# Seven block products in place of eight for the input products of seven expert groups, with weight bounds on ScalarE and the weight clamp on GpSimd

## The chip, the cores and the metric

The kernel runs on one core of a Trainium2 chip. The metric is the device time of one execution, in microseconds. In the profile PE is TensorE's matmul, PEld its weight load, DVE VectorE, ACT ScalarE, POOL GpSimd and SP SyncE.

## What is computed

```python
# 4 x 8 heads, 576 positions, 64 wide; log_f = log(clip(f, 1e-4, 1)), cum = cumsum(log_f)
scores = q @ k.T / 8 + cum[:, None] - cum[None, :]          # causal
x = softmax(scores) @ v                                     # -> 2304 tokens x 512
h = ((x @ w_a) * (x @ w_b)) @ w_out                         # 512 -> 1536 -> 512
u = h @ w_in                                                # 512 -> 2048
g = where(u >= 1, u, where(u <= -1, 0, (u + 1) ** 2 / 4))
out = g @ w_out2                                            # 2048 -> 512
```

All inputs are float32, and the weights come to 68 units of 128 x 512 values, seen by the kernel as pairs of 32-bit words.

## The kernel before, in words

**Precision.** A factor of a matmul in the two expert layers is kept as two float16 parts, high and low. A product is then three matmuls (`mm3`): high x high, high x low and low x high. Tokens are the moving columns, weights the stationary 128 x 128 blocks. The inputs of a layer stand in `xhl` (high `xh`, low `xl`; 4 blocks of 128 rows, 2304 columns), the layer's result is gathered in `y` in float32.

**Groups.** The first layer has six groups of 256 of its 1536 inner columns. A group uses six units of weights: four for the input products (`w_a`, `w_b`), two for the output products. The second layer has four groups of 512 inner columns, with four input and four output units. Group 0 of the first layer is done batch by batch among the attention; its last batch and all other groups make up the late part, which is planned and issued by itself (`late`).

**Items.** In the late part a group goes over the tokens in five spans of 460 or 464 columns (`WSPANS`). An item makes the input products of a span, turns them into activations (for the first layer scale on ScalarE, product on VectorE; for the second clamp on VectorE, square on ScalarE, maximum on VectorE; then on both a float16 copy and its float32 image on ScalarE and the low part by a subtraction on GpSimd, tile `al`), and leaves its output products pending, to be put among the input products of the next item. Output products are added into `y` by VectorE.

**Weights.** `weight_stream` makes float16 parts of the weights two units at a time: a load, magnitude and low word on ScalarE, a clamp, a shift and a combining instruction on VectorE, an addition on GpSimd (`decode`, tile `wm`); then the largest magnitude by VectorE (`wmx`), its square, a matmul with ones and a scale (`norm`); then high part on ScalarE, scaling and low part on GpSimd (`split_unit`), for output units also a scaled-down copy on VectorE. Two `wm` tiles alternate, and finished units lie in rings, input and output ones apart, whose slots come free after a group's last span.

**Order.** The class `Plan` collects all instructions with their dependences (a matrix of PSUM counts as one bank), ranks them by modelled durations, and issues each engine's list in the order that its simulated clock gives; it models that GpSimd and some VectorE instructions exclude each other. Each engine then works through its list in order. All instructions are issued from one line of that class, so every row of the profile names L326 and tiles tell them apart; tiles of the late part have an l in front.

Of the kernel before, what the change touches and what calls it, by code (L numbers as in the profile page):

```python
# [31 lines left out]
WIDE = 464  # L32
# [5 lines left out]
WSPANS = [(460 * i, 460) for i in range(4)] + [(1840, 464)]  # L38
# [5 lines left out]
RI2, RO2 = 4, 4  # L44
LT = 2
# [15 lines left out]
def weight_order():  # L61
    order = []
    for f0, f1 in G1:
        for f in range(f0, f1):
            for n in ("moe_w_a", "moe_w_b"):
                order += [(n, kc, f) for kc in range(KC)]
# [281 lines left out]
def tile_decay_attention__then__moe__then__moe2(  # L348
# [9 lines left out]
    nc.nc_inputs = {qk.tensor.name, v.tensor.name, f.tensor.name, w.tensor.name}  # L358
# [11 lines left out]
    ring_i = Ring(pool("ring_i", 1), RI)  # L370
# [35 lines left out]
    ysc = const.tile([P, len(WSPANS)], F32, name="ysc")  # L406
    yinv = const.tile([P, len(WSPANS)], F32, name="yinv")
# [91 lines left out]
    free = {"in": RI, "out": RO, "next": 0}  # L499
    slots = {"in": [ring_i] * RI, "out": [ring_o] * RO}  # L500
    rings = {"in": slots["in"][:], "out": slots["out"][:]}
    split = {"in": 0, "out": 0}

    def kind(u):
        n = len(G1) * 6
        return "in" if (u % 6 if u < n else (u - n) % 8) < 4 else "out"
# [32 lines left out]
    def norm(sq, inv, sc):  # L539

        bp = psum_t()
        nc.tensor.matmul(bp[:, 0:2], lhsT=unit, rhs=sq, start=True, stop=True)
        nc.vector.tensor_scalar(inv.bitcast(I32), bp[:, 0:2].bitcast(I32), 1, 0x3F800000, ALU.logical_shift_right,
                                ALU.bitwise_and)
        nc.gpsimd.tensor_scalar(inv, inv, 2.0 ** 49, 2.0 ** -76, ALU.mult, ALU.max)
# [9 lines left out]
    def decode(u, m):  # L555
# [10 lines left out]
        nc.vector.tensor_scalar(m, m, F64_MIN, F64_MAX, ALU.max, ALU.min)  # L566
# [9 lines left out]
    def split_unit(u, m):  # L576
# [4 lines left out]
        p = slot(k)  # L581
        hi = p.tile([P, UB, P], F16, name=f"whi_{k}", tag=f"whi_{k}")
        lo = p.tile([P, UB, P], F16, name=f"wlo_{k}", tag=f"wlo_{k}")
# [10 lines left out]
        yield True  # L594

    def weight_stream():
# [5 lines left out]
        for u0 in range(0, NU + 2, 2):  # L602
# [7 lines left out]
            if scaled:  # L610
                norm(sq, winv[:, cols], wsc[:, cols])
                yield True
            if u0 > 0:
                for j in range(2):
                    yield from split_unit(u0 - 2 + j, old[:, j])
            if u0 < NU:
                mx = const2.tile([P, 2], F32, name="wmx", tag="wmx")
                nc.vector.tensor_reduce(mx, new, axis=AX.X, op=ALU.max, apply_absolute_value=True)
                sq = const2.tile([P, 2], BF16, name="wsq", tag="wsq")
                nc.scalar.activation(sq, mx, AF.Square)  # L620
# [13 lines left out]

    def w_free(u):
# [3 lines left out]
        free[kind(u)] += 1  # L639
# [16 lines left out]
    def act_pair(nt):  # L656
        return tuple(env["act"].tile([P, env["width"]], F16, name=n, tag=n)[:, :nt] for n in ("ah", "al"))
# [39 lines left out]
    def group1(g):  # L697

        if ("g", g) not in xw:
# [4 lines left out]
            for i in range(2):  # L704
                nc.gpsimd.tensor_tensor(q[:, 2 * i:2 * i + 2], winv[:, u + 2 * i:u + 2 * i + 2], inv, ALU.mult)
                nc.gpsimd.tensor_scalar(r[:, i:i + 1], q[:, 2 * i:2 * i + 1], q[:, 2 * i + 1:2 * i + 2], 2.0 ** -22,
# [4 lines left out]
    def out_scale1(g, b):  # L711
        if ("o", g, b) not in xw:
            u = base1[g] // UB + 4
            t, o = small("ot", 2), small("os", 2)
            nc.gpsimd.tensor_scalar(t, group1(g)[0], xinv[:, b:b + 1], 2.0 ** 31, ALU.mult, ALU.mult)
            nc.gpsimd.tensor_scalar(t[:, 0:1], t[:, 0:1], t[:, 1:2], 2.0 ** -4, ALU.mult, ALU.mult)
# [4 lines left out]
    def group2(g):  # L721
        if ("k", g) not in xw:
# [3 lines left out]
            nc.vector.tensor_scalar(k, k, 2.0 ** 36, None, ALU.mult)  # L726
# [3 lines left out]
    def moe1_item(g, b, c0, nt, last_use):  # L730
# [5 lines left out]
        def epilogue(oa, ob, r):  # L736
# [3 lines left out]
            nc.scalar.activation(asb, oa, AF.Copy, scale=2.0 ** -26)  # L740
# [34 lines left out]
        def accumulate(c, o, sc):  # L775
            ys = y[:, c, cs]
            if g == 0:
                nc.scalar.activation(ys, o, AF.Copy, scale=sc)
                return
            nc.vector.scalar_tensor_tensor(ys, o, sc, ys, ALU.mult, ALU.add)  # L780
            if g == len(G1) - 1:
                nc.vector.tensor_reduce(ymx[:, c:c + 1], ys, axis=AX.X, op=ALU.max, apply_absolute_value=True)
                if c == KC - 1:
                    finish(ymx)

        def finish(ymx):
            i = WSPANS.index((c0, nt))
            mx = const2.tile([P, 1], F32, name="ymx", tag="ymx")
            box = []
            nc.vector.tensor_reduce(mx, ymx, axis=AX.X, op=ALU.max)  # L790
            after(4, lambda: box.append(top_of(mx, 1)))
            after(9, lambda: spread(box[0], 1, yinv[:, i:i + 1], ysc[:, i:i + 1]))
# [517 lines left out]
```

## Time and profile before

| | |
|---|---|
| median of 3 runs | 1010.12 us (1008.34 to 1010.54) |
| profiled execution | 1009.84 us |
| its span, first to last instruction | 1008.1 us |
| granted TensorE clock, mean over the span | 0.997 |
| TensorE, VectorE, ScalarE, GpSimd busy | 99%, 68%, 59%, 62% |
| late part | 260 to 1004.3 us |

A matmul's record lasts longer than the time until the next one starts, since matmuls overlap; from start to start is what one takes. A duration of VectorE or GpSimd holds the time for which the instruction was held up inside the engine.

### The profile page before, as it was taken

To read this page: it belongs to the slowest core of one execution; us is meant where nothing else is said; L and a number is where in the kernel's file an instruction comes from. 1 tells how busy PE (TensorE), PEld (TensorE's weight loads), DVE (VectorE), ACT (ScalarE), POOL (GpSimd) and SP (SyncE) were. 2 spreads that over 40 slices of the span, in tenths; PEclk is the share of its full clock that TensorE was granted. 3 is DMA by queue.
4 is the path that set the end of the run, shared out by engine and by line. 5 is a ranking of instruction groups with operands and counts; after the bars stand their busy time and mean duration, and the time that the engine had idled before them with its cause. 6 is when DMAs were issued, how large, how long until landed. Compare 5 with 4: busy or idle time off the path is not lost.

```text
span 1008.1 us, 18407 instructions
## 1 busy us (share of the span) xinstructions
PE 993.8 (99%) x6877; PEld 585.7 (58%) x6877; DVE 689.0 (68%) x1570; ACT 594.9 (59%) x1137; POOL 620.8 (62%) x743
## 2 busy tenths in 40 slices
PE   8999999999999999999999999999999999999998
PEld 6888788888754555555555555454555555555554
DVE  7998988778553753755635778987566688487443
ACT  6899989877653442434524445777564556364342
POOL 7689988984672642644624645658574587278321
PEclk8999999999999999999999999999999999999999
DMA  8765555420120210211101121011111112010112
GB/s 230 193 200 157 153 165 160 141 76 10 42 64 21 84 43 1 84 43 42 61 24 42 64 63 43 22 63 38 47 42 42 42 43 63 22 42 11 48 57 76
DMA packets 22114, 72.17 MB, mean 72 GB/s; under 512 B 2772, under 2 KB 5332, under 8 KB 21960
## 3 DMA queue, kind: packets, MB, share of 16 engines
q1 hardware_dynamic: 22024, 70.99, 23.3%
q8 instruction: 54, 0.88, 0.4%
q14 instruction: 36, 0.29, 0.1%
HBM read 60.41 MB, written 5.96 MB: 66 GB/s over the span
## 4 chain that ended last, share of the span: by engine, by line
PE 88%; ACT 4%; DVE 4%; POOL 2%; issue 1%; DMA 0%; ACTq 0%; POOLq 0%; DVEq 0%
PE lmm L326 73%; PE mm L326 4%; PE s L326 4%; PE tp L326 3%; PE o L326 3%; ACT prob L326 1%; ACT th L326 1%; DVE prob L326 1%; DVE tl L326 1%; PE mm L1192 1%; DVE wm L326 1%; POOL qk L326 1%; POOL q L326 0%; DVE xt L326 0%; POOL wm L326 0%
## 5 line engine op out<-in xcount | busy, mean ns | idle before, releaser
L326 POOL TENSOR_TENSOR lal<-ltmp,ltmp 128x460 f16<-128x460 f32 (+2 forms) x134 | 162.1, 1218 | 208.9 <-ACT ltmp L326 192.6
L326 PE MATMUL lmm<-xhl,lwhi_in 128*128 128x460 f16 (+1 forms) x800 | 215.4, 357 | 0.0
L326 PE MATMUL lmm<-xhl,whi_in 128*128 128x460 f16 (+2 forms) x704 | 183.6, 351 | 0.9 <-ACT y L326 0.6
L326 PEld LDWEIGHTS <-whi_in 128*128 128x128 f16 x896 | 86.7, 98 | 70.3 <-issue 2.3
L326 PEld LDWEIGHTS <-lwhi_in 128*128 128x128 f16 x800 | 77.8, 97 | 75.5
L326 DVE TENSOR_SCALAR wm<-wm 128x512 f32<-128x512 f32 (+1 forms) x136 | 93.4, 691 | 33.7 <-ACT wm L326 32.6
L326 PE MATMUL lmm<-lah,lwhi_out 128*128 128x460 f16 (+1 forms) x360 | 115.5, 358 | 0.0
L326 PE MATMUL lmm<-lah,lwlo_out 128*128 128x460 f16 (+1 forms) x360 | 114.8, 358 | 0.0
L326 PE MATMUL lmm<-lal,lwdown 128*128 128x460 f16 (+1 forms) x360 | 114.7, 357 | 0.0
L326 PE MATMUL lmm<-xhl,lwlo_in 128*128 128x460 f16 (+1 forms) x400 | 114.3, 357 | 0.0
L326 POOL TENSOR_TENSOR wm<-wm,wr 128x512 int32<-128x512 int32 x68 | 90.8, 1335 | 36.5 <-DVE wm L326 24.9
L326 ACT ACTIVATE ltmp<-ltmp,lhmid,lihalf 128x460 f32<-128x460 f32 (+1 forms) x80 | 59.9, 766 | 89.8 <-DVE ltmp L326 85.3
L326 ACT ACTIVATE lah<-ltmp 128x460 f16<-128x460 f32 (+2 forms) x134 | 76.6, 578 | 56.1 <-DVE ltmp L326 47.5
L326 DVE SCALAR_TENSOR_TENSOR y<-lmm,los,y 128x460 f32<-128x460 f32 (+1 forms) x100 | 68.2, 692 | 50.3 <-PE lmm L326 50.2
L326 PE MATMUL lmm<-xhl,wlo_in 128*128 128x460 f16 (+2 forms) x352 | 98.5, 351 | 0.0
L326 DVE TENSOR_SCALAR ltmp<-lmm,lhtop,lhlow 128x460 f32<-128x460 f32 (+1 forms) x80 | 58.8, 751 | 52.7 <-PE lmm L326 47.7
L326 ACT ACTIVATE prob<-prob,nm 128x256 f32<-128x256 f32 (+4 forms) x144 | 79.8, 588 | 9.6 <-DVE nm L326 9.4
L326 DVE SCALAR_TENSOR_TENSOR tl<-tp,th 128x384 f16<-128x384 f32 (+2 forms) x128 | 71.4, 567 | 11.0 <-ACT th L326 9.8
L326 ACT ACTIVATE ltmp<-lmm 128x460 f32<-128x460 f32 (+2 forms) x54 | 29.3, 542 | 82.5 <-PE lmm L326 82.3
L326 ACT ACTIVATE ltmp<-lah 128x460 f32<-128x460 f16 (+2 forms) x134 | 75.3, 576 | 2.1
L326 ACT ACTIVATE wr<-wraw 128x512 int32<-128x512 uint32 x68 | 45.8, 673 | 52.1 <-POOL wm L326 51.9
L326 DVE SCALAR_TENSOR_TENSOR ltmp<-lmm,lgr,ltmp 128x460 f32<-128x460 f32 (+2 forms) x54 | 36.2, 680 | 56.5 <-PE lmm L326 52.6
(170 smaller groups left out, 2258.8 us busy)
## 6 DMA issues: line engine op xcount, KB each, us to landing
wraw<-in_w_dram SPq DMA_DIRECT2D x68, 512.0 KB, 3.6
raw<-in_qk_dram SPq DMA_DIRECT2D x26, 608.0 KB, 4.0
vraw<-in_v_dram SPq DMA_DIRECT2D x16, 320.0 KB
qk<-q SPq DMA_DIRECT2D x28, 160.0 KB, 2.4
out_dram<-ltmp SPq DMA_DIRECT2D x16, 230.0 KB, 2.0
y<-in_qk_dram SPq DMA_DIRECT2D x2, 608.0 KB
cum_d<-xhl SPq DMA_DIRECT2D x1, 1216.0 KB
out_dram<-ltmp SPq DMA_DIRECT2D x4, 232.0 KB, 2.0
```

Of the source, the lines that this page charges most:

```text
L326: getattr(getattr(self.nc, engine), method)(*a, **kw)
L1192: nc.heat = lambda: tc.nc.tensor.matmul(heat, lhsT=mask[:, 0:P], rhs=mask[:, 0:512 - HALF], start=False, stop=False, skip_group_check=True)
```

## The change

**Seven products.** The input products of first-layer groups 2 to 5 and second-layer groups 1 to 3 are made by the Strassen-Winograd scheme (`s_set`). A pair of input units is a 2 x 2 arrangement of blocks (two inner blocks by two halves of the 512 rows), and the tokens of an item form the other 2 x 2 arrangement: the same row halves by two column halves, a left one of 384 tokens in the first 1152 and a right one of 384 in the second. Eight block products become seven, of sums of blocks. The sums of weights are made in `split_pair` (four additions on VectorE, more columns of high and low parts), those of the inputs in `x_sums`, once for the first layer during group 1 and once for the second during its group 0; one of them overwrites its place in `xhl`. In a set two partial sums are kept in PSUM: bank X is copied to bank Y by ScalarE while TensorE makes another product in V; V is copied to SBUF by ScalarE; VectorE writes X plus that copy into Z, later into V; TensorE goes on adding into X, Y and Z. The other late groups use `plain_set`, with the same items.

**Items of 768 tokens.** There are three items a group, each two halves of 384 columns, in place of five spans. Seven PSUM banks serve matmuls and one the small transposes and bounds, before six and two. The first layer's two halves of activations share a tile; 18 such tiles and 8 temporaries stand in the late part, before 8 and 8 of single parts and 6.

**Bounds and clamp.** From unit 8 on, a weight's bound is the root of its sum of squares, by ScalarE with an accumulated output, in place of VectorE's maximum, and the clamp of a decoded weight runs on GpSimd. The bound of `y` is likewise from squares. For pairs one bound holds for both units. Scale constants change with that, and one multiplication by 0.25 is added per batch in `xscale`.

**Buffers.** Late input weights lie in four pair tiles (one in place of the early input ring), output units in five slots instead of six.

```diff
-WIDE = 464
+SH = 384
...
-WSPANS = [(460 * i, 460) for i in range(4)] + [(1840, 464)]
+NI = NT // (2 * SH)
...
-RI2, RO2 = 4, 4
-LT = 2
+NPW, RO2 = 4, 3
+SG1, SG2 = 2, 1
+LATE = 8
+LT = 1
+NACT, NTMP = 18, 8
...
+        units = [(n, f) for f in range(f0, f1) for n in ("moe_w_a", "moe_w_b")]
+        for n, f in units if f0 < NEARLY * 2 else sorted(units):
+            order += [(n, kc, f) for kc in range(KC)]
...
-        return "in" if (u % 6 if u < n else (u - n) % 8) < 4 else "out"
+        if u < 6 * NEARLY and u % 6 < 4:
+            return "in"
+        return "pair" if (u % 6 if u < n else (u - n) % 8) < 4 else "out"
+
+    def seven(u):
+        n = len(G1) * 6
+        return u // 6 >= SG1 if u < n else (u - n) // 8 >= SG2
...
-        nc.vector.tensor_scalar(m, m, F64_MIN, F64_MAX, ALU.max, ALU.min)
+        (nc.vector if u < LATE else nc.gpsimd).tensor_scalar(m, m, F64_MAX, F64_MIN, ALU.min, ALU.max)
...
+    def split_pair(u, m):
+        while not free["pair"]:
+            yield False
+        free["pair"] -= 1
+        hl = late_p["pair"][late_p["next"] % NPW]
+        late_p["next"] += 1
+        hi, lo = hl[:, 0], hl[:, 1]
+        sc = wsc[:, u:u + 1]
+        t = m.rearrange("p a (j n) -> p (a j) n", j=2)
+        nc.gpsimd.tensor_scalar(t, t, sc, 0.0, ALU.mult, ALU.add)
+        if not seven(u):
+            nc.scalar.copy(hi[:, 0:4], t)
+            for j in range(2):
+                k = slice(2 * j, 2 * j + 2)
+                nc.gpsimd.tensor_tensor(lo[:, k], t[:, k], hi[:, k], ALU.subtract)
+            ws[u] = ws[u + 1] = (hi, lo)
+            return
+        nc.scalar.copy(hi[:, 0:2], t[:, 0:2])
+        nc.scalar.copy(hi[:, 2], t[:, 3])
+        nc.gpsimd.tensor_tensor(lo[:, 0:2], t[:, 0:2], hi[:, 0:2], ALU.subtract)
+        nc.gpsimd.tensor_tensor(lo[:, 2], t[:, 3], hi[:, 2], ALU.subtract)
+        yield True
+        nc.vector.tensor_tensor(t[:, 3], t[:, 2], t[:, 3], ALU.add)
+        nc.vector.tensor_tensor(t[:, 2], t[:, 0], t[:, 2], ALU.subtract)
+        nc.vector.tensor_tensor(t[:, 0], t[:, 3], t[:, 0], ALU.subtract)
+        nc.vector.tensor_tensor(t[:, 1], t[:, 1], t[:, 0], ALU.subtract)
+        yield True
+        nc.scalar.copy(hi[:, 3:7], t)
+        for j in range(2):
+            k = slice(2 * j, 2 * j + 2)
+            nc.gpsimd.tensor_tensor(lo[:, 3 + 2 * j:5 + 2 * j], t[:, k], hi[:, 3 + 2 * j:5 + 2 * j], ALU.subtract)
+        yield True
+        ws[u] = ws[u + 1] = (hi, lo)
...
+                if u0 < LATE:
+                    nc.vector.tensor_reduce(mx, new, axis=AX.X, op=ALU.max, apply_absolute_value=True)
+                    nc.scalar.activation(sq, mx, AF.Square)
+                else:
+                    squares = wdec_p.tile([P, UB * P], I32, name="wr", tag="wr", bufs=1).bitcast(BF16)
+                if u0 < LATE:
+                    pass
+                elif kind(u0) == "pair":
+                    nc.scalar.activation(squares, new.rearrange("p a n -> p (a n)"), AF.Square, accum_out=mx[:, 0:1])
+                    nc.scalar.copy(sq, mx[:, 0:1].to_broadcast([P, 2]))
+                else:
+                    for j in range(2):
+                        nc.scalar.activation(squares[:, 0:UB * P], new[:, j], AF.Square, accum_out=mx[:, j:j + 1])
+                    nc.scalar.copy(sq, mx)
...
-        return tuple(env["act"].tile([P, env["width"]], F16, name=n, tag=n)[:, :nt] for n in ("ah", "al"))
+        t = env["act"].tile([P, 2 * env["width"]], F16, name="act", tag="act")
+        return t[:, 0:nt], t[:, env["width"]:env["width"] + nt]
...
+    def x_sums(i, second):
+        left, right, own = parts(i)
+        xs = late_p["xs"]
+        for k in range(2):
+            t1, t2, t4 = ((xs[:, 0, n, k, own], xs[:, 1, n, k, own]) for n in range(3))
+            t3 = (xh[:, k, right], xl[:, k, right])
+            sc = ysc[:, i:i + 1]
+            def store(t, d):
+                if second:
+                    nc.scalar.activation(t[0], d, AF.Copy, scale=sc)
+                    nc.vector.scalar_tensor_tensor(t[1], d, sc, t[0], ALU.mult, ALU.subtract)
+                else:
+                    nc.scalar.copy(t[0], d)
+                    nc.vector.tensor_tensor(t[1], d, t[0], ALU.subtract)
+            if second:
+                d1, d2, d3 = (spare() for _ in range(3))
+                y11, y12, y21, y22 = (y[:, kc, cs] for kc in (k, 2 + k) for cs in (left, right))
+                nc.gpsimd.tensor_tensor(d1, y12, y11, ALU.subtract)
+                store(t1, d1)
+                nc.vector.tensor_tensor(d2, y22, y12, ALU.subtract)
+                store(t3, d2)
+                nc.vector.tensor_tensor(d3, d2, y11, ALU.add)
+                store(t2, d3)
+                nc.vector.tensor_tensor(d1, y21, d3, ALU.subtract)
+                store(t4, d1)
+                continue
+            d1, d2, e = spare(), spare(), spare()
+            (h11, l11), (h12, l12), (h21, l21), (h22, l22) = (
+                (xh[:, kc, cs], xl[:, kc, cs]) for kc in (k, 2 + k) for cs in (left, right))
+            nc.vector.tensor_tensor(d1, h12, h11, ALU.subtract)
+            nc.gpsimd.tensor_tensor(e, l12, l11, ALU.subtract)
+            nc.vector.tensor_tensor(d1, d1, e, ALU.add)
+            store(t1, d1)
+            nc.vector.tensor_tensor(d2, h22, h12, ALU.subtract)
+            nc.gpsimd.tensor_tensor(e, l22, l12, ALU.subtract)
+            nc.vector.tensor_tensor(d2, d2, e, ALU.add)
+            store(t3, d2)
+            nc.vector.tensor_tensor(d2, d2, h11, ALU.add)
+            nc.vector.tensor_tensor(d2, d2, l11, ALU.add)
+            store(t2, d2)
+            nc.vector.tensor_tensor(d1, h21, d2, ALU.subtract)
+            nc.vector.tensor_tensor(d1, d1, l21, ALU.add)
+            store(t4, d1)
...
+    def plain_set(pair, i):
+        hi, lo = pair
+        res = []
+        for f in range(2):
+            for h, cs in enumerate(parts(i)[0:2]):
+                o = psum()[:, :SH]
+                for kc in range(KC):
+                    at = slice(kc % 2 * P, kc % 2 * P + P)
+                    wh, wl = (a[:, 2 * f + kc // 2, at] for a in (hi, lo))
+                    mm3(o, (wh, wl, wh), xh[:, kc, cs], xl[:, kc, cs], kc == 0, kc == KC - 1)
+                res.append(((f, h), o))
+        return res
+    def in_set(u, i):
+        return (s_set if seven(u) else plain_set)(w_pair(u), i)
+    def s_set(pair, i):
+        hi, lo = pair
+        left, right, own = parts(i)
+        xs = late_p["xs"]
+        b11, b12, b21, b22 = ([(xh[:, k0 + k, cs], xl[:, k0 + k, cs]) for k in range(2)] for k0 in (0, 2) for cs in (left, right))
+        t1, t2, t4 = ([(xs[:, 0, n, k, own], xs[:, 1, n, k, own]) for k in range(2)] for n in range(3))
+        X, V, Y, Z = (psum()[:, :SH] for _ in range(4))
+        def prod(o, w, xv, first):
+            for k, (h, l) in enumerate(xv):
+                wh, wl = (a[:, w, k * P:(k + 1) * P] for a in (hi, lo))
+                for j, (a, b) in enumerate(((wh, h), (wl, h), (wh, l))):
+                    nc.tensor.matmul(o, lhsT=a, rhs=b, start=first and k + j == 0, stop=k + j == 3, skip_group_check=True)
+        prod(X, 0, b11, True)
+        prod(V, 6, t1, True)
+        nc.scalar.copy(Y, X)
+        vs = tmp(SH)
+        nc.scalar.copy(vs, V)
+        prod(X, 3, t2, False)
+        prod(Y, 1, b21, False)
+        nc.vector.tensor_tensor(Z, X, vs, ALU.add)
+        prod(X, 5, b12, False)
+        prod(Z, 4, b22, False)
+        nc.vector.tensor_tensor(V, X, vs, ALU.add)
+        prod(X, 2, t4, False)
+        return (((0, 0), Y), ((0, 1), Z), ((1, 1), V), ((1, 0), X))
...
+    def out_of(u, n, acts, i, last, accumulate):
+        for h in range(2):
             for c in range(KC):
-                o = slice(c0, c0 + nt)
-                after(11 + 2 * c, lambda c=c: nc.scalar.activation(xh[:, c, o], y[:, c, o], AF.Copy, scale=ysc[:, i:i + 1]))
-                after(12 + 2 * c, lambda c=c: nc.vector.scalar_tensor_tensor(
-                    xl[:, c, o], y[:, c, o], ysc[:, i:i + 1], xh[:, c, o], ALU.mult, ALU.subtract))
-
-        ymx = const2.tile([P, KC], F32, name="ymx4", tag="ymx4") if g == len(G1) - 1 else None
+                o = psum()[:, :SH]
+                for m in range(n):
+                    mm3(o, w_block(u * UB + c * n + m), acts[m, h][0], acts[m, h][1], m == 0, m == n - 1)
+                accumulate(c, h, o)
+                if last and h == 1 and (c + 1) * n % UB == 0:
+                    w_free(u + c * n // UB)
+    def s1_item(g, i):
+        u, last = 6 * g, i == NI - 1
+        cs = parts(i)[0:2]
+        asb, acts = {}, {}
+        for key, o in in_set(u, i):
+            asb[key] = tmp(SH)
+            nc.scalar.activation(asb[key], o, AF.Copy, scale=2.0 ** -18)
+        if last:
+            free_pair(u)
+        flush_all()
+        for key, o in in_set(u + 2, i):
+            p = tmp(SH)
+            ah, al = act_pair(SH)
+            acts[key] = ah, al
+            nc.vector.scalar_tensor_tensor(p, o, 2.0 ** -14, asb[key], ALU.mult, ALU.mult)
+            nc.scalar.activation(ah, p, AF.Copy, scale=1.0 / LOW)
+            nc.scalar.activation(asb[key], ah, AF.Copy, scale=LOW)
+            nc.gpsimd.tensor_tensor(al, p, asb[key], ALU.subtract)
+        if last:
+            free_pair(u + 2)
+        if g == SG1 - 1:
+            x_sums(i, False)
...
+                norm([sq[:, j:j + 1] for j in range(2 * KC)], yinv[:, i:i + 1], ysc[:, i:i + 1], 2)
+                sy = ysc[:, i:i + 1]
+                for kc, c in ((0, 0), (1, 0), (2, 0), (3, 0), (2, 1), (3, 1)) + ((0, 1), (1, 1)) * (SG2 > 0):
+                    nc.scalar.activation(xh[:, kc, cs[c]], y[:, kc, cs[c]], AF.Copy, scale=sy)
+                    nc.vector.scalar_tensor_tensor(xl[:, kc, cs[c]], y[:, kc, cs[c]], sy, xh[:, kc, cs[c]], ALU.mult, ALU.subtract)
+                if SG2 == 0:
+                    x_sums(i, True)
...
+        if g == SG2 - 1:
+            x_sums(i, True)
...
+        nc.vector.tensor_scalar(sb, sb, 0.25, None, ALU.mult)
...
+        free["pair"] = NPW
+        pairs = pool("ring_pair", 1)
+        late_p["pair"] = [pairs.tile([P, 2, 7, 2 * P], F16, name=f"whl{j}") for j in range(NPW - 1)]
+        late_p["pair"].append(ring_in.rearrange("p u a (b n) -> p (u a b n)", b=2)[:, 0:14 * 2 * P].rearrange(
+            "p (a b n) -> p a b n", a=2, b=7))
+        late_p["next"] = 0
+        late_p["xs"] = pool("xs", 1).tile([P, 2, 3, 2, NI * SH], F16, name="xs")
...
+        for g in range(NEARLY, len(G1)):
+            for i in range(NI):
+                if g == SG1 == NEARLY:
+                    for j in range(i and i + 1, min(i + 2, NI)):
+                        x_sums(j, False)
+                s1_item(g, i)
+                pump()
+        for g in range(len(G2)):
+            for i in range(NI):
+                s2_item(g, i)
+                pump()
+        flush_all()
```

## Rows read from the trace of the kernel before

**Rows 1.** Page, part 1: busy time, share of the span and instructions.

```profile
PE 993.8 (99%) x6877; PEld 585.7 (58%) x6877; DVE 689.0 (68%) x1570; ACT 594.9 (59%) x1137; POOL 620.8 (62%) x743
```

**Rows 2.** Busy time by stretch: length; PE, PEld, DVE, ACT, POOL; PEclk, DMA share, GB/s.

```profile
0.00:100.00 100.00, 93.47 (x1029) 76.61 (x1031) 88.92 (x290) 86.02 (x179) 81.48 (x102) 0.97 0.68 193
100.00:200.00 100.00, 97.68 (x1223) 82.12 (x1220) 88.52 (x287) 90.01 (x196) 91.18 (x91) 1.00 0.51 154
200.00:260.00 60.00, 58.63 (x735) 48.99 (x733) 43.78 (x147) 45.63 (x98) 37.65 (x45) 1.00 0.15 44
260.00:1004.30 744.30, 743.98 (x3904) 378.00 (x3903) 467.06 (x848) 373.19 (x668) 410.53 (x508) 1.00 0.15 46
```

**Rows 3.** Chain that ended last: start us, us, what.

```profile
677.34 0.64 ACT y L326
...
684.85 0.68 ACT wm L326
...
685.55 0.66 DVE wm L326
...
686.68 45.50 PE lmm L326 x233
...
926.61 77.67 PE lmm L326 x399
...
1004.30 0.70 DVE ltmp L326
```

**Rows 4.** Timeline of TensorE: start us, us, what; four like rows left out.

```profile
279.82 0.29 PE L326 MATMUL lmm<-lal,wdown 128*128 128x288 f16 x1
...
280.43 0.36 PE L326 MATMUL lmm<-xhl,lwhi_in 128*128 128x460 f16 x1
```

**Rows 5.** Tile wm (weights being decoded): duration ns min/median/max.

```profile
L326 DVE TENSOR_SCALAR wm<-wm x136: 394/448/1721, 24.5 to 911.2; 128x512 f32<-128x512 f32 x68, 128x512 int32<-128x512 int32 x68
...
L326 DVE SCALAR_TENSOR_TENSOR wm<-wraw,wm x68: 671/692/1750, 32.1 to 913.2; 128x512 int32<-128x512 int32 x68
L326 POOL TENSOR_TENSOR wm<-wm,wr x68: 1258/1272/1722, 39.9 to 914.3; 128x512 int32<-128x512 int32 x68
L326 POOL TENSOR_SCALAR wm<-wm,wsc x68: 682/697/1131, 82.1 to 929.3; 128x512 f32<-128x512 f32 x68
L326 DVE TENSOR_REDUCE wmx<-wm x34: 1202/1210/1221, 48.8 to 915.6; 128x2 f32<-128x1024 f32 x34
...
L326 POOL TENSOR_TENSOR lwlo_out<-wm,lwhi_out x18: 1152/1162/1600, 290.2 to 931.1; 128x512 f16<-128x512 f32 x18
```

**Rows 6.** By operation and shape: busy us, mean ns; idle before, releasers.

```profile
L326 PE MATMUL lmm<-xhl,lwhi_in 128*128 128x460 f16 x640 | 167.4, 357 | 0.0
...
L326 DVE SCALAR_TENSOR_TENSOR y<-lmm,los,y 128x460 f32<-128x460 f32 x80 | 54.6, 691 | 47.1 <-PE lmm L326 47.1
...
L326 DVE TENSOR_SCALAR wm<-wm 128x512 f32<-128x512 f32 x68 | 44.7, 657 | 32.7 <-ACT wm L326 32.6
...
L326 ACT ACTIVATE ltmp<-lmm 128x460 f32<-128x460 f32 x40 | 22.1, 552 | 74.2 <-PE lmm L326 74.0
...
L326 ACT ACTIVATE junk<-vraw 128x640 f16<-128x640 f32 x16 | 11.8, 737 | 1.7 <-DMA vraw<-in_v_dram 1.7
```

**Rows 7.** Timelines of GpSimd and of VectorE, 842 to 850 us.

```profile
842.15 3.76 POOL L326 TENSOR_TENSOR lal<-ltmp,ltmp 128x460 f16<-128x460 f32 x3
845.88 1.72 POOL L326 TENSOR_TENSOR wm<-wm,wr 128x512 int32<-128x512 int32 x1
...
849.44 1.17 POOL L326 TENSOR_TENSOR lal<-ltmp,ltmp 128x460 f16<-128x460 f32 x1 [1.20 <-ACT ltmp L326]
...
844.83 1.64 DVE L326 SCALAR_TENSOR_TENSOR wm<-wraw,wm 128x512 int32<-128x512 int32 x1
```

More of the change, by code (lines that the diff above doesn't have):

```diff
@@ L633, in w_block, with w_pair @@
         return tuple(t[:, i % UB, :] for t in ws[u])
+    def w_pair(u):
+        while u not in ws:
+            assert w_pump()
+        return ws[u]
     def w_free(u):
@@ L638, in w_free @@
         free["next"] += 1
-        free[kind(u)] += 1
+        free[kind(u)] += 1 if kind(u) != "pair" else u % 2
     def mm3(o, wb, xh, xl, first, last):
@@ L808, in moe2_item, with s2_item @@
+    def s2_item(g, i):
+        u0, last = len(G1) * 6 + 8 * g, i == NI - 1
+        nm = 4
+        cs = parts(i)[0:2]
+        w_pair(u0)
+        w_pair(u0 + 2)
         ih, ihalf, top, low, full, osc = (small(n, 4) for n in ("ih", "ihalf", "htop", "hlow", "hfull", "hos"))
@@ L864, in finish @@
[L864 to L885 removed]
+        acts = {}
@@ new lines, in s2_item @@
+        for p in range(2):
+            for (f, h), o in in_set(u0 + 2 * p, i):
+                t, r = tmp(SH), tmp(SH)
+                ah, al = act_pair(SH)
+                acts[2 * p + f, h] = ah, al
+                m = slice(2 * p + f, 2 * p + f + 1)
+                nc.vector.tensor_scalar(t, o, top[:, m], low[:, m], ALU.min, ALU.max)
+                nc.scalar.activation(t, t, AF.Square, scale=ihalf[:, m], bias=mid)
+                nc.vector.scalar_tensor_tensor(r, o, full[:, m], t, ALU.mult, ALU.max)
+                nc.scalar.activation(ah, r, AF.Copy, scale=1.0 / LOW)
+                nc.scalar.activation(t, ah, AF.Copy, scale=LOW)
+                nc.gpsimd.tensor_tensor(al, r, t, ALU.subtract)
+            if last:
+                free_pair(u0 + 2 * p)
+            if p == 0:
+                flush_all()
@@ L1169, in late @@
         env["ps"] = Ring(pool("ps_m2", 1, space=bass.MemoryType.PSUM), 8 - LT, "l")
-        env["width"] = WIDE
-        env["act"] = Ring(pool("act2", 1), 8, "l")
-        env["tmp"] = Ring(pool("tmp2", 1, side="right"), 6, "l")
-        last = [(B - 1, (B - 1) * S + n * HALF, HALF) for n in range(2)]
-        spans = [(B - 1, *sp) for sp in WSPANS]
-        items = [(moe1_item, g, *sp, sp == last[-1]) for g in range(NEARLY) for sp in last]
-        for item, groups in ((moe1_item, range(NEARLY, len(G1))), (moe2_item, range(len(G2)))):
-            items += [(item, g, *sp, sp == spans[-1]) for g in groups for sp in spans]
-        for item, *args in items:
-            for _ in item(*args):
-                tick()
-                if clock[0] % 2 == 0 or free["in"] + free["out"] > 5:
-                    w_pump()
-        drain()
-        for _ in flush():
-            tick()
-        drain()
+        env["width"] = SH
+        env["act"] = Ring(pool("act2", 1), NACT, "l")
+        env["tmp"] = Ring(pool("tmp2", 1, side="right"), NTMP, "l")
+        for g in range(NEARLY):
+            for n in range(2):
+                for _ in moe1_item(g, B - 1, (B - 1) * S + n * HALF, HALF, n == 1):
+                    tick()
+        drain()
+        for g in range(NEARLY, len(G1)):
[9 more added lines that the diff above has]
+                pump()
+        flush_all()
     nc.vector.memset(warm, 1.0)
```

208 lines of the change are left out of this document (94 added, 114 removed).

## The prediction

> **What bounds the kernel now.** I read the busy shares first, then the same by stretch, then the chain that ended last, then the durations by operation. The page puts TensorE at 99% of the span, the other three at 62 to 68% [rows 1]. By stretch [rows 2] there are two parts. Up to 260 us (attention and the first expert group) all four engines are 80 to 98% busy. From 260 to 1004.3 us (the late part, where the whole change lies) TensorE is busy 743.98 of 744.30 us, VectorE 467, ScalarE 373, GpSimd 411, and the granted clock is 1.00, the 2.4 GHz level. The chain [rows 3] is TensorE in that part, with one excursion at 677 to 687 us that runs through other engines although TensorE has work at the same time; then one VectorE instruction and a store end it. So a microsecond of matmul taken out of the late part is a microsecond of the end, as long as the rest can feed TensorE faster.
>
> **How long a matmul takes.** The late part holds 3904 TensorE instructions [rows 2]. The code says which: 72 per 460-column span in each of five first-layer groups and 96 in each of four second-layer groups, five spans each, so 3720, of which a fifth are 464 wide (460.8 on average); 144 of 288 columns; the rest tiny ones for bounds. A busy time of 357 ns for 460 columns is no cost, since matmuls overlap. What counts is start to start. At 288 columns it is 0.122 us (from 279.82 to 280.43 five steps) [rows 4]. For 460.8 columns it follows from the part's length: (744.3 - 144 x 0.122 - about 2 for the tiny ones)/3720 = 0.1947 us; the last chain piece, 399 in 77.67 us, gives the same [rows 3]. On the line between these two, 384 columns take 0.122 + 96/172.8 x 0.0727 = 0.1624 us; in proportion to 460.8 it would be 0.1623, so narrower tiles cost nothing here.
>
> **What the change removes from TensorE.** With 384 columns and two halves, a plain input set (2 x 2 blocks of weights) is 48 matmuls, a seven-product one 42. A first-layer group is three items of 96 + 48 matmuls, plain, or 84 + 48; a second-layer one three items of 96 + 96, or 84 + 96. So 432 + 4 x 396 + 576 + 3 x 540 = 4212. TensorE's late work goes from 3720 x 0.1947 = 724.3 to 4212 x 0.1624 = 684.0 us: **40 us less**. The 144 narrow ones stay.
>
> **What it adds elsewhere, in the late part** (durations without waiting, [rows 5, 6]). GpSimd: 58 clamps moved to it at 0.70 = 41; 14 seven-product pairs with 768 more columns of the low-part subtraction, 1.16 x 1.5 = 1.7 each, 24; 18 subtractions for the input sums, 1.0 each; fewer small scale instructions (12 items for 20), -15. So 411 becomes about 475. VectorE loses 58 clamps (0.66 with waits) and 28 maxima of 1.21, about -72, and 14 for the old maxima of y; it gains 84 additions out of PSUM (0.69 x 384/460 = 0.58) = 49, 56 weight additions of 256 columns (0.67/2 = 0.34) = 19, 114 operations for the input sums (0.67 x 384/512 = 0.50) = 57, and 13 for narrower tiles with more fixed cost: about 520 and longer waits. ScalarE gains the squares (18 of 1024 columns and 26 of 512, from 0.74 for 640: about 40 with the small copies), 84 copies of 384 columns (0.55 at 460, so 0.48) = 40, 48 for the input sums = 24, the sums of weights 15, y's squares 12: 373 becomes about 500. All three stay under 75% of 704 us, so on averages TensorE remains the bound.
>
> **What the averages hide.** VectorE and GpSimd delay each other here. The shift of a decoded weight takes 394 ns at best, 1721 at worst; the combining instruction with two inputs 671 and 1750 [rows 5]. One case shows why: the combining instruction starts at 844.83 and lasts 1.64 us, until GpSimd's row of three subtractions is over at 845.91 plus 0.56; GpSimd's next, 845.88, takes 1.72 for a usual 1.27 [rows 7]. So I count as shared time all of GpSimd, and of VectorE the shift, what reads two operands from SBUF, and the scaled-down copies (at most the shift's 0.39). The late part before: 411 + 58 x 1.45 + 20 = 514 of 744, 69%, and TensorE lost nothing by it. After: decode 3.03 a unit (0.70 + 1.27 + 0.39 + 0.67), a plain pair 3.6, a seven-product pair 1.3 + 3.5 x 1.16 + 4 x 0.34 = 6.7, an output unit 2.1, a subtraction of activations 0.98 (1.17 x 384/460 [rows 7]), the input sums 24 x 0.50 + 4 x 0.98 = 15.9 an item the first time and 14 x 0.5 + 2 x 0.98 = 9 the second: 58 x 3.03 + 4 x 3.6 + 14 x 6.7 + 26 x 2.1 + 156 + 75 + 42 = 612 of 704, 87%.
>
> It is uneven. From 260 us to the start of the third late first-layer group TensorE has 144 x 0.122 + 432 x 0.1624 + 396 x 0.1624 = 152 us of work. Due in it: 12 decodes 36, pairs 34, four output units 8, activations 27, all three first input sums 48, small 3: 156. The second such stretch is the last first-layer group and the first of the second layer, 158 us, with 170 of shared time, 18 of it due only later. An ordinary second-layer group has 76 of 88, where before it was 71 of 93.
>
> The Trainium skill speaks against the change here: SBUF — State Buffer, section "Who interferes with whom", says the port that VectorE's second read shares with GpSimd is an exclusive lock, and the loser blocks for the whole instruction. This trace agrees, with the 1.64 us above. By that rule, with the port packed to 90% in the two full stretches, the sum would be 1002 us.
>
> **Waits added (W).** The fullest that I count in the kernel before is 71 of 93 us, 76%, so bounds: in the first stretch 156 - 152 = 4 us at perfect packing, though the last pair is due up to 11 us later, so 0; at 90% packing 156/0.9 - 152 = 21. In the second, 0 to (170 - 18)/0.9 - 158 = 11. I take 8 and 3, nearer the low ends: many instructions in the count have slack of tens of us, and the four pair buffers let weights be made a group ahead. The new waits inside a seven-product set are costed at nothing: TensorE must wait for the copy of X, then for two additions, but six matmuls of another product, 0.97 us, stand in each gap. Against that stand 0.48 to 0.58 for the instruction, 0.16 by which a matmul's record outlasts its step (0.357 - 0.195), and two handovers that the chain shows as 0.02 each (684.85 + 0.68 to 685.55; 926.61 + 77.67 to 1004.30) [rows 3]: at most 0.78. Cover gone, each of the three gaps would cost that.
>
> Costed at nothing too: the earlier part. It changes by two clamps that move to a GpSimd that is 81 to 91% busy, one more small multiply per batch, and a merged pair of tiles; its order is made anew by the same planner, so +-2 us either way. Weight loads: DMA is 15% busy late [rows 2]. PSUM: seven banks for matmuls instead of six, four of them taken by a set; the other three hold output products. The end stays: one evacuation and a store.
>
> **Sum.** The profiled execution took 1009.84 us, 1.7 beside its span of 1008.1, and lies 0.3 under the median of the runs. 1009.84 - 40.3 + 11 = 980.5, with the 0.3 **981 us**. Its own range, W from 0 to 20: 969 to 990.
>
> **Rivals.**
> *Shared port binds two stretches*: W of 20 to 38, 990 to 1008 us. For it: 156 and 170 us of demand in 152 and 158, and delays of over 1 us in single instructions now. Against: slack ahead of most due times; the list order weighs the port. Worked out: 21 + 11 = 32 gives 1002.
> *The set's handovers are not covered*: slower than before. VectorE at about 75%, its instructions 0.6 to 1.2 us long and in order, so an addition due within 0.97 us can stand behind another. All three gaps bare, 3 x 0.78 = 2.3 us in each of 42 sets, 98 us on 970: 1068. It decides from 40/42 = 0.95 us a set. Against: other matmuls (output products of the item before, the next set's first products in three free banks) can stand in the gaps.
> *Nothing gained*: another engine already sets the pace at some places, so shorter TensorE work only uncovers it. Against: 0.3 us of idle time in 744. It would take W = 40 by chance: 1010.
>
> **Chances.** Forecast 0.62; below 969 through a better order of the early part 0.04; port 0.25; nothing gained 0.02; handovers, slower 0.07. A measurement of this kernel tells about 0.2% (2 us) from no change. Faster 0.91, same 0.02, slower 0.07. The range 969 to 1000 leaves out some 0.04 below, 0.08 of the port's case above, and the 0.09 beyond.
>
> **What the next profile shows if this is right.** Late part from about 260 us; 4212 wide matmuls in it, 384 columns, start to start 0.162; its length near 715 us; TensorE's idle time some 10 us, most before the third and the first second-layer group, released by VectorE or GpSimd; GpSimd some 470 us busy late, VectorE 520 and above with the port's waits, ScalarE 500. Waits of TensorE on ScalarE's copies or VectorE's additions spread over all 42 sets would speak for the handovers; VectorE rows of two SBUF operands at 1 us and more, with TensorE idle in just the two full stretches, for the port. An early part longer by over 3 us, or a clock under 1.00 late, would upset the sum from outside it.

## The result

The changed kernel takes 983.25 us (median; 981.08 to 984.11), the kernel before 1009.89 in the same comparison: a ratio of 0.9735, 95% interval 0.9715 to 0.9755. Run again beside other kernels it gave 981.38, 0.9731 (0.9712 to 0.9749). The prediction was 981.

The page of the changed kernel, busy time by engine, against [rows 1]:

```profile
PE 955.1 (97%) x7372; PEld 630.9 (64%) x7372; DVE 762.1 (78%) x1727; ACT 708.0 (72%) x1492; POOL 696.9 (71%) x792
```

Its busy time by stretch, columns as in [rows 2]; the late part ends with TensorE's last matmul at 977.3:

```profile
0.00:260.00 260.00, 246.82 (x2962) 204.69 (x2963) 225.66 (x724) 221.42 (x470) 211.03 (x238) 1.00 0.50 144
260.00:977.30 717.30, 708.26 (x4410) 426.25 (x4409) 535.79 (x1002) 486.62 (x1024) 485.84 (x554) 1.00 0.15 48
```

The late part is 717.3 us long where it was 744.3 [rows 2]; that is the whole difference. It starts where it did, the end behind it (3.4 us) is about what it was (3.8), and the clock stays at the 2.4 GHz level. Of the 717.3, matmuls account for 4212 x 0.1624 + 144 x 0.122 + some 2 = 703.6, so **13.7 us is waiting**. The busy sum shows only 9.0 us of it as idle, because a record of 326 ns covers a gap of up to 0.16 us to the next one.

In 20 us there is room for some 125 matmuls; stretches with fewer show where TensorE waited. The same columns, TensorE first:

```profile
360.00:380.00 20.00, 19.43 (x118) 11.05 (x116) 16.43 (x32) 9.23 (x21) 10.95 (x12) 1.00 0.00 1
380.00:400.00 20.00, 20.00 (x126) 12.05 (x124) 18.83 (x38) 12.29 (x26) 9.68 (x10) 1.00 0.17 54
400.00:420.00 20.00, 18.61 (x114) 10.71 (x113) 13.59 (x26) 12.01 (x25) 16.70 (x19) 1.00 0.17 53
420.00:440.00 20.00, 18.36 (x111) 10.39 (x110) 14.68 (x25) 14.94 (x32) 16.53 (x17) 1.00 0.34 106
600.00:620.00 20.00, 18.77 (x123) 11.16 (x122) 17.20 (x39) 19.73 (x51) 14.62 (x20) 1.00 0.04 17
720.00:740.00 20.00, 17.59 (x107) 9.78 (x105) 18.21 (x36) 18.65 (x41) 16.80 (x23) 1.00 0.16 52
740.00:760.00 20.00, 20.00 (x125) 12.03 (x123) 13.96 (x29) 10.92 (x23) 14.87 (x20) 1.00 0.22 62
```

From 360 to 440 us some (7 + 11 + 14) x 0.1624 = 5.2 us is missing, from 720 to 740 some 2.9: in the first two seven-product groups of the first layer and in the first of the second layer. Most of the late part between looks like 740 to 760. The busy share of VectorE alone (third number of a row after the length, 18.83 of 20 us from 380 to 400) does not mark these places: there it is 94% and nothing is missing, from 400 to 440 it is 71% and 4 us are. The largest waits of TensorE in the late part (engine, tile, for whom: us in all, times, longest):

```profile
PE lmm L329 <- DVE lmm L329: 3.7, 4, 1.8
PE lmm L329 <- ACT xhl L329: 1.2, 1, 1.2
PE lmm L329 <- ACT lmm L329: 1.2, 1, 1.2
PE lmm L329 <- ACT whi L329: 1.1, 1, 1.1
```

The first is an addition out of PSUM, the third a copy inside a set; both are handovers that the prediction costed at nothing. The second is a copy of new inputs for the second layer, the fourth high parts of output weights that come late. The longest, in the timelines of TensorE and VectorE:

```profile
723.81 1.95 PE L329 MATMUL lmm<-xs,whl 128*128 128x384 f16 x11
725.60 1.14 PE L329 MATMUL lmm<-xhl,whl 128*128 128x384 f16 x6
728.56 0.65 PE L329 MATMUL lmm<-xhl,whl 128*128 128x384 f16 x3 [1.82 <-DVE lmm L329]
...
725.15 0.68 DVE L329 TENSOR_SCALAR ltmp<-lmm,lhtop,lhlow 128x384 f32<-128x384 f32 x1
725.74 0.15 DVE L329 TENSOR_SCALAR winv<-ltp 128x2 int32<-128x2 int32 x1
725.81 0.61 DVE L329 SCALAR_TENSOR_TENSOR ltmp<-lmm,lhfull,ltmp 128x384 f32<-128x384 f32 x1
726.33 0.51 DVE L329 TENSOR_SCALAR wm<-wm 128x512 int32<-128x512 int32 x1
726.77 0.61 DVE L329 SCALAR_TENSOR_TENSOR ltmp<-lmm,lhfull,ltmp 128x384 f32<-128x384 f32 x1
727.30 0.68 DVE L329 SCALAR_TENSOR_TENSOR wm<-wraw,wm 128x512 int32<-128x512 int32 x1
727.89 0.15 DVE L329 RECIPROCAL wsc<-winv 128x2 f32<-128x2 f32 x1
727.97 0.54 DVE L329 TENSOR_TENSOR lmm<-lmm,ltmp 128x384 f32<-128x384 f32 x1
```

The product into X is over at 725.76. The addition that reads it could have started then, but it stands in VectorE's list behind a clamp, bounds, two maxima and two steps of weight decoding, and starts at 727.97. The six matmuls of cover are done at 726.74; TensorE is idle until 728.56. Of the seven instructions in front GpSimd slows only the shift, and that by 0.1 us (0.51 for 0.41 at best).

### The profile page after: what moved, and what is told of

Same layout as the page of the kernel before. It is cut to its first block, busy times and chain, and to the rows that moved or that the text cites. A ratio compares the mean times of both kernels' runs of the same rounds, so it can differ in the third digit from the quotient of the medians.

```text
span 980.7 us, 19992 instructions
## 1 busy us (share of the span) xinstructions
PE 955.1 (97%) x7372; PEld 630.9 (64%) x7372; DVE 762.1 (78%) x1727; ACT 708.0 (72%) x1492; POOL 696.9 (71%) x792
## 4 chain that ended last, share of the span: by engine, by line
PE 75%; ACT 9%; DVE 6%; POOL 3%; DMA 3%; issue 2%; DVEq 0%; SPq 0%; ACTq 0%; POOLq 0%
PE lmm L329 63%; PE mm L329 4%; PE tp L329 3%; PE s L329 3%; PE o L329 2%; DVE ltmp L329 2%; ACT prob L329 2%; ACT th L329 1%; DMA qk<-cum_d 1%; DMA raw<-in_qk_dram 1%; ACT ltmp L329 1%; ACT wr L329 1%; DVE wm L329 1%; POOL wm L329 1%; DVE xhl L329 1%
## 5 line engine op out<-in xcount | busy, mean ns | idle before, releaser
L329 PE MATMUL lmm<-xhl,whl 128*128 128x384 f16 x1224 | 272.2, 326 | 5.2 <-DVE lmm L329 3.7
L329 PEld LDWEIGHTS <-whl 128*128 128x128 f16 x1818 | 176.6, 98 | 122.5 <-issue 7.2
L329 POOL TENSOR_TENSOR lact<-ltmp,ltmp 128x384 f16<-128x384 f32 (+1 forms) x160 | 167.8, 1057 | 108.9 <-ACT ltmp L329 92.5
L329 PE MATMUL lmm<-xs,whl 128*128 128x384 f16 x594 | 129.0, 326 | 0.0
L329 PE MATMUL lmm<-lact,lwdown 128*128 128x384 f16 x384 | 116.7, 326 | 0.2 <-POOL lact L329 0.2
L329 PEld LDWEIGHTS <-ring_in 128*128 128x128 f16 x906 | 86.5, 98 | 45.5 <-issue 3.2
L329 PE MATMUL lmm<-lact,lwlo 128*128 128x384 f16 x384 | 115.5, 326 | 0.2
L329 PE MATMUL lmm<-lact,lwhi 128*128 128x384 f16 x384 | 115.2, 326 | 0.4
L329 PE MATMUL lmm<-xhl,ring_in 128*128 128x384 f16 (+1 forms) x456 | 104.4, 317 | 0.6 <-ACT y L329 0.6
L329 ACT ACTIVATE lact<-ltmp 128x384 f16<-128x384 f32 (+1 forms) x160 | 80.9, 514 | 29.2 <-DVE ltmp L329 28.7
```

The costliest lines, as they stand in the source:

```text
L329: getattr(getattr(self.nc, engine), method)(*a, **kw)
```

## The experiments

Each is an edit of the changed kernel, timed beside the kernel before; runs 1 to 4, 5 to 8 and 9 to 12 shared a chip each. Ratios are to the kernel before, with 95% intervals. The planner orders every edited kernel anew, so the lists differ by more than the edit. The profiles allow a second comparison: in every version with 4212 wide matmuls the late part has 4410 TensorE instructions, and its length from the first to the last of them leaves out the early part, whose end lies between 258 and 263 us. In the changed kernel that length is 717.18 us, in its second profile (run 12) 716.71.

**1. All late input products by eight.**

```diff
-SG1, SG2 = 2, 1
+SG1, SG2 = 7, 5
```

> All late input products by eight block products, everything else of the change kept (items of 2 x 384 columns, pair buffers, bounds by squares on ScalarE, clamp on GpSimd); the input sums fall away with the sets. Theory (the gain is the 252 matmuls alone): 4464 matmuls of 0.1624 us, 725 us, some 2 us of waits as in the kernel before: 1010 us, 1007 to 1013. Rival (tiles, bounds or clamp bring part of the gain themselves): under 1004.

1012.6 us, ratio 1.0026 (1.0014 to 1.0039). Its late part:

```profile
260.00:1005.00 745.00, 744.47 (x4659) 451.72 (x4659) 391.52 (x746) 428.14 (x863) 425.96 (x508) 1.00 0.14 45
```

TensorE is without work for 0.5 us, and the last piece of the chain, 405 matmuls in 65.83 us, gives 0.1625 each, the price the prediction had by interpolation. So tiles, bounds, clamp and buffers gain nothing by themselves; by the medians they even cost some 2.7 us, by the late part of the profiled executions 1.1 (745.45 against 744.35), of which 4464 x 0.1624 against 3720 x 0.1947 explains 0.7. The whole gain is the 252 matmuls.

**2. Sets without handovers.**

```diff
-        nc.scalar.copy(Y, X)
-        vs = tmp(SH)
-        nc.scalar.copy(vs, V)
         prod(X, 3, t2, False)
-        prod(Y, 1, b21, False)
-        nc.vector.tensor_tensor(Z, X, vs, ALU.add)
+        prod(Y, 1, b21, True)
         prod(X, 5, b12, False)
-        prod(Z, 4, b22, False)
-        nc.vector.tensor_tensor(V, X, vs, ALU.add)
+        prod(Z, 4, b22, True)
```

> Seven-product sets whose four banks are independent: the copies of X and V and the two additions are left out, so the input products of those groups are partial sums only. 4212 matmuls as in the changed kernel. Theory (some 14 us of waits come mostly from the time that VectorE and GpSimd share, in the stretches with input sums): 978 to 982, and TensorE still waits some 4 us or more between 360 and 440 us. Rival (waits inside the sets): 970 to 974, waits gone everywhere.

969.68 us, ratio 0.9607 (0.9592 to 0.9621): the rival's time, against my theory. The stretch 340 to 440 us without handovers, and below it in the changed kernel:

```profile
340.00:440.00 100.00, 100.00 (x622) 60.20 (x620) 76.48 (x140) 57.16 (x118) 73.01 (x75) 1.00 0.18 53
```

```profile
340.00:440.00 100.00, 96.40 (x586) 56.23 (x585) 81.66 (x148) 61.51 (x130) 64.95 (x67) 1.00 0.17 53
```

All input sums and all weight pairs are still made. VectorE, without the additions of the sets, has 76 us of work instead of 82, GpSimd 73 instead of 65, and TensorE misses nothing. Demand on what they share does not of itself hold TensorE up. The time is also 40.2 us under the kernel before: the matmuls' term, bare.

**3. Input sums left out.** `x_sums` keeps only

```diff
+            for n, t in enumerate((t1, t2, t4)):
+                nc.scalar.copy(t[0], xh[:, k, left if n else right])
+                nc.scalar.copy(t[1], xl[:, k, left if n else right])
```

> Input sums replaced by plain copies of single blocks on ScalarE, so the 114 VectorE and 18 GpSimd instructions of the sums are left out (the products are of unsummed inputs); 4212 matmuls and all handovers kept. Theory (shared time in the stretches with input sums): 974 to 978, TensorE's waits between 360 and 440 and between 600 and 640 us nearly gone (7 us in the changed kernel). Rival (handovers inside the sets): 982 to 984, waits as before.

974.38 us, ratio 0.9657 (0.9641 to 0.9674): the theory's time. The stretch:

```profile
340.00:440.00 100.00, 99.92 (x618) 59.68 (x617) 58.05 (x114) 57.44 (x116) 57.77 (x66) 1.00 0.13 43
```

VectorE 58 us instead of 82, and with all handovers in place the waits of this stretch are nearly gone. Runs 2 and 3 together say that it takes both: a handover on TensorE's path, and a list in which it stands behind other work. Leaving out the sums takes away VectorE's work and demand on what VectorE and GpSimd share at once, so this run does not tell which of the two matters.

**4. Clamp back on VectorE.**

```diff
-        (nc.vector if u < LATE else nc.gpsimd).tensor_scalar(m, m, F64_MAX, F64_MIN, ALU.min, ALU.max)
+        nc.vector.tensor_scalar(m, m, F64_MAX, F64_MIN, ALU.min, ALU.max)
```

> Only the clamp of decoded weights goes back to VectorE for all units. Theory (time shared by VectorE and GpSimd is what is scarce): 58 x (0.70 - 0.39) = 18 us less of it, so 980 to 983, same or a little faster than the changed kernel. Rival (VectorE's queue is what is scarce): 58 more instructions on it, 984 to 988.

984.7 us, ratio 0.9745 (0.9725 to 0.9764): not to be told from the changed kernel.

**5. The load of the handovers without their waits.**

```diff
-        nc.scalar.copy(Y, X)
         vs = tmp(SH)
-        nc.scalar.copy(vs, V)
+        for _ in range(2):
+            nc.scalar.copy(vs, V)
...
-        nc.vector.tensor_tensor(Z, X, vs, ALU.add)
+        nc.vector.tensor_tensor(vs, V, vs, ALU.add)
...
```

> The two copies and two additions of a set are made at full width, but all read bank V, which TensorE has finished, and write SBUF, so TensorE waits for none of them inside a set; input sums kept; the products are partial sums only. The run without handovers left out both the waiting and 84 + 84 instructions, which this one tells apart. Theory (an addition or copy that TensorE needs stands behind other instructions in a loaded queue): no waits, 969 to 972. Rival (the load alone delays what TensorE needs elsewhere): 977 to 983.

972.57 us, ratio 0.9643 (0.9625 to 0.9661). VectorE has 549 us of work from 260 to 965 us here, more than the changed kernel's 532, and the time falls by 0.0092 of 1009, 9 us. Of the 13 us by which the ratios put run 2 below the changed kernel, some 3.6 are left here. The late parts agree; in order, the changed kernel, run 2 and this run:

```profile
260.09:977.27 717.18, 708.26 (x4410) 426.25 (x4409) 535.76 (x1002) 486.53 (x1023) 485.84 (x554) 1.00 0.15 48
260.69:964.64 703.95, 703.87 (x4410) 427.31 (x4409) 501.55 (x918) 453.65 (x939) 495.19 (x554) 1.00 0.15 48
261.12:968.12 707.00, 704.77 (x4410) 427.09 (x4409) 551.71 (x1002) 487.42 (x1023) 491.75 (x554) 1.00 0.15 48
```

The changed kernel lies 13.2 us above run 2, the load without the waiting 3.1.

**6. The waits of the handovers without their load.** Copies and additions cover one column:

```diff
+        one = slice(0, 1)
-        nc.scalar.copy(Y, X)
+        nc.scalar.copy(Y[:, one], X[:, one])
...
-        nc.vector.tensor_tensor(Z, X, vs, ALU.add)
+        nc.vector.tensor_tensor(Z[:, one], X[:, one], vs[:, one], ALU.add)
...
```

> The handovers stay where they are, but the two copies and two additions cover one column of 384; input sums kept; the products are partial sums only. It takes some 0.4 us from each of the 168 instructions (about 33 us from VectorE, 26 from ScalarE) and keeps the waiting. Theory: a short instruction still stands behind the queue, so waits remain in the stretch with input sums, 974 to 980. Rival (load alone): waits gone, 969 to 972.

975.76 us, ratio 0.9681 (0.9655 to 0.9707), its own runs 974.06 to 979.86. Its late part:

```profile
261.85:970.29 708.44, 706.14 (x4410) 426.77 (x4409) 515.04 (x1002) 464.20 (x1023) 488.88 (x554) 1.00 0.15 48
```

Waiting remains although the instructions waited for are short: 4.5 us over run 2 in the late part (by the ratios 7, but these also hold the early part, and the runs lie 6 us apart). So the load alone leaves 3.1 us, the waiting alone 4.5, and only the two together 13.2. Neither is shown to be the larger part, and at least 13.2 - 3.1 - 4.5 = 5.6 us need both, a wait and a list made longer by the work of the sets themselves.

**7. Bounds back on VectorE.**

```diff
-                    nc.scalar.activation(squares, new.rearrange("p a n -> p (a n)"), AF.Square, accum_out=mx[:, 0:1])
-                    nc.scalar.copy(sq, mx[:, 0:1].to_broadcast([P, 2]))
+                    nc.vector.tensor_reduce(mx[:, 0:1], new.rearrange("p a n -> p (a n)"), axis=AX.X, op=ALU.max, apply_absolute_value=True)
+                    nc.scalar.activation(sq, mx[:, 0:1].to_broadcast([P, 2]), AF.Square)
...
```

> Bounds of weights by VectorE's maximum again (some 30 instructions of 1.2 us), no squares on ScalarE; the clamp stays on GpSimd. Theory (VectorE's queue delays the handovers): 36 us more on VectorE, instructions of 1.2 us in front of additions, 986 to 994. Rival (ScalarE's copies are what is late): ScalarE loses 40 us, 978 to 983.

980.83 us, ratio 0.9723 (0.9697 to 0.9749). My theory expected 986 and more; some 30 us more on VectorE (561.5 from 260 to 970 us against 532.5) and 26 less on ScalarE (460.1 against 486.6) cost nothing. Output units are treated likewise in lines not shown.

**8. More passes of the planner.**

```diff
-SWEEPS = (20, 8)
+SWEEPS = (20, 40)
```

> The same instructions; the planner makes 40 passes over the late part in place of 8, and takes the best order it has seen. If the waits come from the order of the lists, a better order takes some of the 14 us away: 977 to 982. If they come from demand that no order meets, or from times that the planner's model has wrong: 982 to 985, as the changed kernel.

980.28 us, ratio 0.9729 (0.9705 to 0.9752). Not told apart from the changed kernel. Between 340 and 440 us TensorE's busy time is 96.40 as in the changed kernel, so more passes found nothing better there. The late part of its profile is 714.71 us, 2.0 to 2.5 below the changed kernel's two: differences of that size between the other runs can be the order's.

**9. First sums one group later.**

```diff
-SG1, SG2 = 2, 1
+SG1, SG2 = 3, 1
```

> Seven products only from first-layer group 3 on, so the first input sums are made during group 2, away from the first filling of the weight buffers; 36 more matmuls, 5.8 us. Theory (waits near 360 to 440 us come from sums and weight building falling together): those waits, about 5 us, go, and the time is 982 to 985. Rival (the waits go with the sums, wherever they are): they move on by one group, 987 to 990.

984.44 us, ratio 0.9752 (0.9733 to 0.977). The stretch that held the most waits:

```profile
340.00:440.00 100.00, 100.00 (x620) 60.04 (x619) 78.95 (x139) 55.34 (x113) 63.50 (x67) 1.00 0.11 33
440.00:500.00 60.00, 60.00 (x374) 36.08 (x373) 47.10 (x87) 36.84 (x78) 38.07 (x39) 1.00 0.20 63
```

The sums now fall into it, VectorE is 79% busy, and there are no waits, neither in it nor in the first seven-product group behind it. With 36 matmuls (5.8 us) more the median is 3.1 us over the changed kernel beside it. So sums and sets together do not make the waits of the first stretch. That the first filling of the weight buffers is the third thing it takes fits this, but no run varies that filling by itself.

**10. Bounds on VectorE and 40 passes together**, the edits of 7 and 8.

> Bounds of weights by VectorE's maximum, clamp on GpSimd, and 40 passes of the planner. If what each gave singly (2.4 and 3.0 us under the changed kernel's median) is real and adds up: 976 to 979. If it was spread between runs: 981 to 984.

980.0 us, ratio 0.9714 (0.9698 to 0.9731). The lowest median of the versions that compute the whole reference, but its interval meets that of the changed kernel beside it, 0.9712 to 0.9749: no gain shown. Its late part, 714.68 us, is that of runs 7 (714.33) and 8 (714.71), so the two do not add up.

**11. Clamp and bounds both back on VectorE**, the edits of 4 and 7.

> Seven products alone: both the clamp and the bounds of weights on VectorE as before the change, 58 + 30 more instructions there (some 60 us), GpSimd 41 and ScalarE 40 us less. If VectorE's queue is what delays the sets: 985 to 992, and moving work off it was needed. If the engines are interchangeable here, as the two single moves suggest: 980 to 985.

986.79 us, ratio 0.9778 (0.9763 to 0.9792), apart from the changed kernel's. VectorE's load from 260 to 970 us, and below it that of the changed kernel:

```profile
260.00:970.00 710.00, 698.46 (x4353) 421.09 (x4354) 588.26 (x1086) 459.06 (x938) 448.60 (x496) 1.00 0.15 47
```

```profile
260.00:970.00 710.00, 700.99 (x4367) 422.09 (x4367) 532.54 (x996) 486.62 (x1024) 485.84 (x554) 1.00 0.15 47
```

With both parts undone VectorE is 83% busy instead of 75%, and some 5 us are lost by the medians. Only 2.0 to 2.4 of them lie in the late part of the profiles (719.15 us), no more than a new order moved it in run 8; where the rest comes from is not shown. With either part alone no loss can be told (runs 4 and 7).

**12. The changed kernel again**, beside 9 to 11; its result stands at the top.

> The changed kernel beside the other three on the same chip: 983, within 981 to 985.

## Why the prediction was right, and where it was not

**The matmuls' term held.** 40.3 us less was predicted from a line between two widths; 0.1625 us a matmul (run 1) and 40.2 us with the waits gone (run 2) confirm price and sum. That nothing else of the change gains shows in run 1.

**The waits' size held, their cause only in part.** The sum had W = 11 on top of the kernel before; the profile has 13.7 us of waiting in all. The sum put them down to the time that VectorE and GpSimd share, and costed the handovers inside the sets at nothing. Run 2 overturns that step: input sums and weights still made, no handovers, no waits. So it is luck that 11 us for one cause lie so near to 13.7 that need another. By the late parts, 10 of the 13 us go when the handovers' load stays without the waiting (run 5), and 9 when the waiting stays without the load (run 6); at least 5.6 need both. The step's mistake was to set an instruction's own duration (0.58 us) against the cover of 0.97 us on an engine that is 75% busy, 82% from 340 to 440 us, and works in order. What counts is what stands in front of it: 2.2 us at 727.97.

**The shared port does delay instructions; how much of the waiting it makes is open.** The combining instruction of weights is at 669 ns at best and 1777 at worst in the changed kernel, as in [rows 5]; the low part of an input sum takes 546 in the median and up to 1619:

```profile
L329 DVE SCALAR_TENSOR_TENSOR wm<-wraw,wm x68: 669/684/1777, 26.9 to 894.5; 128x512 int32<-128x512 int32 x68
```

```profile
L329 DVE TENSOR_TENSOR xs<-lact,xs x18: 538/546/1619, 264.4 to 397.2; 128x384 f16<-128x384 f32 x18
```

The slowest combining instruction stands in the chain of the wait for a copy inside a set. GpSimd, VectorE, ScalarE and TensorE there:

```profile
399.51 1.26 POOL L329 TENSOR_TENSOR wm<-wm,wr 128x512 int32<-128x512 int32 x1
...
399.54 1.78 DVE L329 SCALAR_TENSOR_TENSOR wm<-wraw,wm 128x512 int32<-128x512 int32 x1
401.24 1.66 DVE L329 SCALAR_TENSOR_TENSOR y<-lmm,los,y 128x384 f32<-128x384 f32 x3
...
400.80 0.67 ACT L329 ACTIVATE wr<-wraw 128x512 int32<-128x512 uint32 x1 [1.67 <-POOL wm L329]
401.88 0.46 ACT L329 COPY lmm<-lmm 128x384 f32<-128x384 f32 x1 [0.41 <-DVE y L329]
...
402.40 1.14 PE L329 MATMUL lmm<-xs,ring_in 128*128 128x384 f16 x6 [1.19 <-ACT lmm L329]
```

The combining instruction lasts 1.1 us longer than at best, until 0.55 us after GpSimd's addition is over, and VectorE's sums into `y`, for which the copy waits, stand behind it. ScalarE was busy with an instruction of its own until 401.47, so at most 0.4 of the 1.2 us is this delay's.

Run 4, which by the prediction's durations makes the shared time 18 us less and VectorE's list longer, changed nothing. How much of VectorE's queueing the port makes over the whole late part was not separated. The rule of the Trainium skill that the prediction weighed (SBUF — State Buffer, "Who interferes with whom") is borne out by single instructions (0.67 against 1.78 us), not by the 1002 us that it gave for the sum.

**Where.** The two stretches named, before the third late group and around the layers' change, do hold waits (360 to 440, 600 to 640 us), though about half of the first lie behind the start of that group, near 406 us. A third at 720 us, the second layer's first sets, was not named. Of the prediction's two signs, waits spread over all 42 sets for the handovers and idle time in just two stretches for the port, the profile shows neither. Runs 3 and 9 show the sums' part in the first stretch.

**The load.** GpSimd was forecast at about 475 us late, VectorE at 520 and more, ScalarE at 500: 486, 536 and 487. Two readings of the rows were off, without weight in the sum: ScalarE is 59% busy before the change, not 62 or more, and from 200 to 260 us the three engines beside TensorE are 63 to 76% busy, not 80 and more. The term of 42 us in the shared time of 612 is nowhere explained.

**The rivals.** The handovers' rival was right in its mechanism and wrong in its size: not 2.3 us in each of 42 sets, but some 10 us in all, in few places; that other matmuls fill most gaps fits this. It stays far from the 0.95 us a set at which it would decide. What makes the remaining 5 us of run 3 over run 2, with the sums gone, was not tried further.

## What to carry to other kernels

Where one engine bounds a long stretch, its removed work times its start-to-start price gives the gain well; then look for new points at which it must wait for another engine, and cost each by what stands in front in that engine's list, not by the instruction itself. To test such a wait, keep its load and drop its dependence, then the reverse; runs that drop both cannot tell. That work moved off a crowded engine matters only near its limit is a guess from one run: here VectorE at 83% lost some 5 us by the medians, 2 in the late part, and at 75 to 79% (changed kernel, runs 4 and 7) none that could be told. Where the time before a change moves between executions, compare the changed part alone in the profiles: in run 11 that leaves 2 of the 5 us, in run 6 4.5 of the 7.

## What was not expected of the hardware

Copies and additions of one column between two products still leave 4.5 us of waits, a third of those of full width (run 6). TensorE's records hide a gap of up to 0.16 us each: 9.0 us of idle time show where counting matmuls gives 13.7. GpSimd's clamp of 512 columns took 0.615 us in the median where 0.70 was taken from its neighbour, VectorE's addition of 256 columns 0.424 where 0.34 was, both in the rows of the tile wm:

```profile
L329 POOL TENSOR_SCALAR wm<-wm x60: 607/615/917, 149.9 to 890.2; 128x512 f32<-128x512 f32 x60
L329 DVE TENSOR_TENSOR wm<-wm x56: 405/424/1485, 317.4 to 883.9; 128x256 f32<-128x256 f32 x56
```
